# Fused attention and two feed-forward blocks: row loads for the norms held behind key loads, queries loaded once to 64 partitions, and the second product of four more pairs in plain float32

## The chip, the cores and the metric

The program runs on one core of a Trainium2 chip. The metric is the device time of one execution in microseconds (us). An engine named PE here is TensorE (matrix products), DVE is VectorE, ACT is ScalarE, POOL is GpSimd, and SP is SyncE, whose queue issues every load and store of this kernel in program order.

## The reference, cut to what matters

```python
batch, n_heads, seq, head_dim = (4, 12, 448, 64)
q_n, k_n = rmsnorm(q, g_q), rmsnorm(k, g_k)          # over head_dim
scores = q_n @ k_n.T / sqrt(head_dim)
attn = softmax(scores)                                # max taken off, sum + 1e-9
x = (attn @ v) -> (batch * seq, 768)
a, b = x @ w1, x @ w2                                 # 768 x 1024 each
x = ((a * b) @ w3) @ w_out                            # 1024 x 1024, 1024 x 768
h = x @ w_in                                          # 768 x 2048
out = (h * clip(h + 3, 0, 6) / 6) @ w_out2            # 2048 x 768
```

The weights arrive as 64-bit floats and are turned into 32-bit ones on the chip.

## The kernel before

**Precision.** A float32 product is made of "fp32r" parts: each operand is split into a rounded high part and the rest (low), and high·high, high·low and low·high are added up (`mm3`, L79 to L82; the three products are its lines L80, L81 and L82; I call the three together a triple). Splitting costs one ACT copy for the high part and one subtraction on DVE or POOL for the low part.

**Work of a pair.** The 48 heads are taken as 24 pairs, six to a batch. A pair has eight score steps: one product of queries and keys of 112 x 448 against both key parts (`score`, L536 and L537), then on DVE the scaling with the row maximum (`scale_max`, L543) and the sign change of the maximum (L550), then the exponential on ACT (L555). Eight steps later the scores are transposed (L562, four to a block of 128 keys), copied out of PSUM by ACT as high part (`thi`, L571) and by DVE as low part (`tlo`, L581), and multiplied with V (`pv`). `vsplit` (L524 ACT, L525 POOL) makes V's parts, so V's two parts and the scores' parts give [V-high, V-low] x high and x low (L614, L615; L602 for the block shared by both heads). `xcopy` (ACT) and `xadd` (L630, DVE) put the two column halves together, and `xout` (POOL) divides by the row sum.

**Full pairs.** For pairs in `FULL` nothing is split: V is loaded straight into the tile that TensorE reads (`load_v`, two buffers, tag `vo`), the scores' transposes are copied once (ACT), and one float32 product per block does the work (L610, and L596 for the shared block). `tlo`, `vsplit` and `xadd` return at once. Before, `FULL` holds pairs 0 and 1.

**Norms.** `load_nat` loads queries and keys row by row (tag `nat`, two buffers); `ssq` squares them (ACT, L436), `ssum` sums them (DVE, L442), and a chain of short DVE and ACT operations (L448 to L466) makes the factors of two pairs, which go to memory and come back spread over all partitions (`load_rb`). `load_q` loads the transposed queries, twice over on 128 partitions (tag `qr`), and `qhi` and `qlo` make the high part on partitions 0 to 63 and the low part on 64 to 127.

**Filler.** Between the score steps `fill` puts in products of the feed-forward part: first W' = w3·w_out (128 triples of 384 columns, 384 matmuls), then from about pair 9 on layer 1 and layer 2 of the batches that attention has finished (triples of 448 columns). `rate` says how much per step. Their weights go through `convert` (L135 ACT, L136, L138 and L141 DVE) and a split (ACT and POOL), with few buffers. After the 24 pairs comes the rest of the feed-forward part.

**What sets the order.** The program says in which step each piece is called (`at(t, ...)` with the offsets of `SHIFT`), but a scheduler at build time fixes the final order on each engine from its own estimates. `tc.issue_after` keeps an instruction behind another one on the same queue; it adds no wait for the data.

Of the kernel before, what the change touches and what calls it, by code (L numbers as in the profile page):

```python
# [12 lines left out]
F32 = mybir.dt.float32  # L13
# [3 lines left out]
AF = mybir.ActivationFunctionType  # L17
# [5 lines left out]
B, H, S, D = 4, 12, 448, 64  # L23
HP = H // 2
NP = B * HP
P = 128
# [9 lines left out]
NH = DM // 2  # L36
XB = 7
TAGS = ("s", "t", "v", "f")
FULL = (0, 1)
LG = 8  # L40
AHEAD = 3
K3 = 12
# [4 lines left out]
def fused_kernel(ctx: ExitStack, tc: tile.TileContext, nat, qT, kT, vin, gq, gk,  # L47
                 w12, w3t, wo, win, wo2, outT):
    nc = tc.nc
# [15 lines left out]
    G = gs[:, 2:3]  # L65
# [21 lines left out]
    def dma(out, src):  # L87
        return nc.sync.dma_start(out, src)
# [7 lines left out]
    def at(t, fn, *a):  # L96
        tasks[max(t + SHIFT.get(getattr(fn, "__name__", ""), 0), now[0])].append((fn, a))
# [304 lines left out]
    T = {}  # L402
    anchors = {}

    def attention(ap, rate):
        def full(i):
            return i in FULL

        def load_nat(i):
            if i < NP:  # L410
                T["nat", i] = ap.tile([CP, 4 * NC, D], F32, tag="nat", bufs=2, name="nat")
                a = T.get(("kl", i - 2))
                with ExitStack() as es:
                    if a is not None:
                        es.enter_context(tc.issue_after(a.ins))
                    dma(T["nat", i], nat[i].rearrange("p a b d -> p (a b) d"))

        def load_q(i):
            T["qr", i] = ap.tile([P, 2, S], F32, tag="qr", bufs=1, name="qr")
            dma(T["qr", i], qT[i])  # L420

        def load_k(i):
            T["kr", i] = ap.tile([P, 2, S], F32, tag="kr", bufs=1, name="kr")
# [78 lines left out]

        def qhi(i):
            T["Q", i] = q = ap.tile([P, 2, S], F32R, tag="Q", bufs=2, name="Q")
            nc.scalar.activation(q, T["qr", i], AF.Copy, scale=G)

        def qlo(i):
            a = slice(64, 128)
            q = T["Q", i]
            nc.vector.scalar_tensor_tensor(out=q[a], in0=T["qr", i][a], scalar=G[a, :], in1=q[a],  # L510
                                           op0=ALU.mult, op1=ALU.subtract)

        def ksplit(i):
# [133 lines left out]
        groups = {s: [s, s + 1] for s in range(0, NP, 2)}  # L647

        load_nat(0)
        load_nat(1)  # L650
        dma(gs[:, 0:1], gq)
        dma(gs[:, 1:2], gk)
        nc.vector.tensor_mul(G, gs[:, 0:1], gs[:, 1:2])
        load_q(0)
        load_k(0)
        open_wprime()
# [10 lines left out]
        first = ExitStack()  # L667
        first.enter_context(tc.issue_after(T["rbl"].ins))
        qhi(0)
        qlo(0)  # L670
        ksplit(0)
        for z in range(10):
            prep[0].step()
        load_q(1)
        load_k(1)
        for z in range(16):
            prep[0].step()
        load_nat(2)
        load_nat(3)

        for i in range(NP):
            t = 8 * i
            n = i + 1
            if n < NP:
                at(t, qhi, n)
                at(t + 1, qlo, n)
                at(t + 2, ksplit, n)
            at(t - 4, load_v, i)
            if i + 2 < NP:
                at(t + 3, load_q, i + 2)  # L690
                at(t + 5, load_k, i + 2)
            at(t + 1, vsplit, i)
            if i % 2 == 0 and i + 2 < NP:
                g = groups[i + 2]
                at(t, ssq, i + 2)
                at(t + 2, ssq, i + 3)
                at(t + 3, ssum, i + 2, g)
                at(t + 3, load_nat, i + 4)
                at(t + 4, ssum, i + 3, g)
                at(t + 4, load_nat, i + 5)  # L700
                at(t + 5, rms1, g)
                at(t + 6, rms2, g)
                at(t + 16, load_rb, i + 3)

            u = t + LG
            at(u + 2, rsum1, i)
            at(u + 6, xcopy, i, 0)
            at(u + 7, xadd, i, 0)
            at(u + 8, small1, i, None)
            at(u + 9, small2, i, None)  # L710
            at(u + 9, xcopy, i, 1)
            at(u + 10, xadd, i, 1)
            at(u + 13, xout, i)
            if i % 2 == 0 and i + 2 < NP:
                g = groups[i + 2]
                tasks[t + LG] = [z for z in tasks[t + LG] if z[0] is not small1]
                tasks[t + LG + 1] = [z for z in tasks[t + LG + 1] if z[0] is not small2]
                at(t + LG, small1, i - 1, g)
                at(t + LG + 1, small2, i - 1, g)

        t = -1
# [36 lines left out]
    with tc.tile_pool(name="att", bufs=2, side="left") as ap:  # L758
        attention(ap, rate)
# [45 lines left out]
    step, q = 0, 0  # L805
# [126 lines left out]
```

## Time and profile before

| | us |
|---|---|
| median of 3 runs (lowest, highest) | 1272.6 (1270.17, 1278.13) |
| the profiled execution, as timed | 1276.18 |
| span of its trace | 1274.3 |

| engine | busy us | share of the span | instructions |
|---|---|---|---|
| PE | 1183.1 | 93% | 5868 |
| PE weight loads | 1033.9 | 81% | 5868 |
| DVE | 795.1 | 62% | 1524 |
| ACT | 678.8 | 53% | 1305 |
| POOL | 463.6 | 36% | 292 |

The span counts from the first to the last instruction; the timed execution holds 1.9 us more around it. Shares are averages over stages with different limits, so the stages have to be read one by one. "PEclk" is the granted clock of TensorE as a share of its upper level, 2.4 GHz; its other level, 1.2 GHz, is 0.5. Busy time of PE counts overlapping matmuls once, and a matmul's own time is longer than the distance to the next start, so a price is read from starts. An fp32 matmul leaves two records in the trace, an fp32r one leaves one.

### The profile page before, as it was taken

Reading aid. Unit: us, or ns where it says so; the run is one execution under the profiler, and the core shown is the slowest. Engines: PE = TensorE matmul, PEld = TensorE weight load, DVE = VectorE, ACT = ScalarE, POOL = GpSimd, SP = SyncE. Lnnn points to the kernel's source line nnn. Section 1 sums busy time; section 2 is a strip of 40 time slices with the busy share of each in tenths; the row PEclk is TensorE's granted clock in tenths of the full one; section 3 lists DMA queues with packets and bytes.
Section 4 is the critical chain, followed back from the end, with each engine's and each line's share of the span. In section 5 each row is a group of like instructions: output and inputs, shape, how many; then the busy total and the mean of one; then the engine's idle time right before and its main releaser. Section 6 shows DMA issues by size and latency. Waiting matters only on the chain.

```text
span 1274.3 us, 16884 instructions
## 1 busy us (share of the span) xinstructions
PE 1183.1 (93%) x5868; PEld 1033.9 (81%) x5868; DVE 795.1 (62%) x1524; ACT 678.8 (53%) x1305; POOL 463.6 (36%) x292
## 2 busy tenths in 40 slices
PE   3587998888889999999999999889999999999998
PEld 2355987667668999999998998778999999999997
DVE  6989789989993578768643446994433343343332
ACT  5887667866783566766642223444533353344332
POOL 4334324624443112222111003445454454545542
PEclk9698998989999999999999999899999999999999
DMA  7898664666688666676349983450100020001001
GB/s 248 253 256 243 202 193 167 194 229 228 211 274 306 209 217 199 235 225 220 134 163 382 348 323 113 158 173 25 60 28 1 1 87 1 1 1 44 1 1 44
DMA packets 64693, 203.72 MB, mean 160 GB/s; under 512 B 8544, under 2 KB 25440, under 8 KB 64608
## 3 DMA queue, kind: packets, MB, share of 16 engines
q1 hardware_dynamic: 64608, 202.65, 48.2%
q8 instruction: 46, 0.75, 0.2%
q14 instruction: 39, 0.32, 0.1%
HBM read 173.93 MB, written 28.68 MB: 159 GB/s over the span
## 4 chain that ended last, share of the span: by engine, by line
PE 67%; DMA 11%; DVE 10%; issue 5%; ACT 3%; POOL 2%; SPq 1%; DVEq 0%; POOLq 0%; ACTq 0%
PE bank L80 8%; PE bank L82 8%; PE bank L81 8%; PE acc L81 6%; PE acc L82 6%; PE acc L80 5%; PE h L80 5%; PE h L81 5%; PE h L82 5%; PE bank L562 3%; DMA raw<-in_w_dram 2%; DVE wf L141 2%; DMA wr<-in_wo_dram 2%; PE bank L536 2%; PE bank L537 2%
## 5 line engine op out<-in xcount | busy, mean ns | idle before, releaser
L800 POOL TENSOR_TENSOR wis<-wf,wis 128x768 fp32r<-128x768 f32 x63 | 119.8, 1902 | 234.1 <-ACT wis L799 234.1
L872 DVE SCALAR_TENSOR_TENSOR u<-u,h 128x448 f32<-128x448 f32 x64 | 39.5, 618 | 217.3 <-ACT u L871 217.3
L800 POOL TENSOR_TENSOR wos<-wf,wos 128x768 fp32r<-128x768 f32 x64 | 119.0, 1860 | 103.6 <-ACT wos L799 103.6
L80 PE MATMUL bank<-xhl,ws 128*128 128x448 f32 x384 | 145.1, 378 | 7.7 <-ACT ws L285 6.3
L543 DVE CUSTOM_DVE_ANT_0 PP<-bank,rb,rq 112x448 f32<-112x448 f32 x192 | 129.1, 677 | 31.9 <-PE bank L537 27.4
L82 PE MATMUL bank<-xhl,ws 128*128 128x448 f32 x384 | 143.9, 375 | 4.9 <-POOL ws L287 4.9
L81 PE MATMUL acc<-g,wos 128*128 128x448 f32 x384 | 144.3, 376 | 3.8 <-DVE g L876 3.7
L555 ACT ACTIVATE PP<-PP,mx 112x448 f32<-112x448 f32 x192 | 127.4, 664 | 37.4 <-DVE mx L550 34.2
L80 PE MATMUL acc<-g,wos 128*128 128x448 f32 x384 | 138.5, 371 | 5.5 <-ACT g L875 5.5
L82 PE MATMUL acc<-g,wos 128*128 128x448 f32 x384 | 143.2, 373 | 0.0
L81 PE MATMUL bank<-xhl,ws 128*128 128x448 f32 x384 | 142.5, 371 | 0.1
L80 PE MATMUL h<-x2h,wis 128*128 128x448 f32 x378 | 139.0, 368 | 0.0
L81 PE MATMUL h<-x2h,wis 128*128 128x448 f32 x378 | 138.9, 368 | 0.0
L82 PE MATMUL h<-x2h,wis 128*128 128x448 f32 x378 | 137.5, 364 | 0.4 <-POOL wis L800 0.4
L876 DVE TENSOR_TENSOR g<-u,g 128x448 fp32r<-128x448 f32 x64 | 97.9, 1529 | 33.6 <-ACT g L875 33.6
L871 ACT ACTIVATE u<-h,half 128x448 f32<-128x448 f32 x64 | 40.4, 631 | 143.2 <-PE h L82 143.2
L536 PE MATMUL bank<-K,Q 128*112 128x448 f32 x192 | 78.3, 409 | 37.5 <-DVE mx L543 25.0
L562 PE MATMUL bank<-ident,PP 112*128 112x112 f32 x672 | 97.0, 267 | 11.8 <-DVE xl L581 10.2
L562 PEld LDWEIGHTS bank<-ident,PP 112*128 112x128 f32 x672 | 80.5, 145 | 33.8 <-DVE xl L581 13.3
L571 ACT ACTIVATE xh<-bank 128x448 fp32r<-128x448 f32 (+1 forms) x156 | 83.0, 537 | 43.3 <-PE bank L562 38.4
L581 DVE TENSOR_TENSOR xl<-bank,xh 128x448 fp32r<-128x448 f32 x142 | 87.1, 615 | 25.5 <-ACT xh L571 23.8
L799 ACT ACTIVATE wos<-wf 128x768 fp32r<-128x768 f32 x64 | 54.1, 846 | 86.9 <-PE acc L82 86.7
(126 smaller groups left out, 2763.5 us busy)
## 6 DMA issues: line engine op xcount, KB each, us to landing
ws<-w12d SPq DMA_DIRECT2D x48, 768.0 KB, 5.1
ws<-wpd SPq DMA_DIRECT2D x32, 768.0 KB, 4.2
raw<-in_w_dram SPq DMA_DIRECT2D x32, 384.0 KB, 4.3
w12d<-ws SPq DMA_DIRECT2D x16, 768.0 KB, 6.0
wr<-in_win_dram SPq DMA_DIRECT2D x16, 768.0 KB, 4.5
wr<-in_wo_dram SPq DMA_DIRECT2D x16, 768.0 KB, 6.6
nat<-in_nat_dram SPq DMA_DIRECT2D x24, 448.0 KB, 5.9
qr<-in_qT_dram SPq DMA_DIRECT2D x24, 448.0 KB, 6.4
```

The source lines that it names most:

```text
L80: nc.tensor.matmul(ps, lh, rh, start=first, stop=False)
L81: nc.tensor.matmul(ps, lh, rl, start=False, stop=False)
L82: return nc.tensor.matmul(ps, ll, rh, start=False, stop=last)
L536: nc.tensor.matmul(ps[:CP, :S], qs, k1[:, j, :], start=True, stop=False)
L543: anchors[8 * i + s].append(nc.vector.tensor_tensor_reduce(out=T["PP", i][:, c, sl], in0=ps[:CP, :S], in1=T["rb", i][:, sl], op0=ALU.mult, ...
L555: anchors[8 * i + s].append(nc.scalar.activation(v, v, AF.Exp, bias=T["m", i][:, 8 + s : 9 + s], accum_out=T["sum", i][:, s : s + 1]))
L562: nc.tensor.transpose(ps[:, c * CP : c * CP + CP], src[:, c, kb * P : kb * P + P], ident[:CP, :CP])
L571: nc.scalar.activation(hi, ps, AF.Copy)
L581: nc.vector.tensor_sub(lo, ps, hi)
L799: nc.scalar.activation(t[:, 0, :], wf[q], AF.Copy)
L800: nc.gpsimd.tensor_sub(t[:, 1, :], wf[q], t[:, 0, :])
L876: nc.vector.tensor_sub(g[:, 1, :], u, g[:, 0, :])
```

## The change

Four edits. `FULL` becomes `range(HP)`, so pairs 2, 3, 4 and 5 are also done in plain float32 (no V split, no low parts, no adding of halves). `load_nat` of a later pair is called three steps later and is put behind a key load on SP's queue; before, the key load it asked for had not been issued yet at that step, and the hold took effect only for pairs 2 and 3. The queries are loaded once, to 64 partitions, and `qlo` reads from partitions 0 to 63 and writes to 64 to 127.

```diff
-FULL = (0, 1)
+FULL = range(HP)
...
         def load_nat(i):
...
-                a = T.get(("kl", i - 2))
+                a = T.get(("kl", i - 2)) or T.get(("kl", i - 3))
...
-            T["qr", i] = ap.tile([P, 2, S], F32, tag="qr", bufs=1, name="qr")
-            dma(T["qr", i], qT[i])
+            T["qr", i] = ap.tile([D, 2, S], F32, tag="qr", bufs=1, name="qr")
+            dma(T["qr", i], qT[i][:D])
...
-            nc.scalar.activation(q, T["qr", i], AF.Copy, scale=G)
+            nc.scalar.activation(q[:D], T["qr", i], AF.Copy, scale=G[:D, :])
...
-            a = slice(64, 128)
             q = T["Q", i]
-            nc.vector.scalar_tensor_tensor(out=q[a], in0=T["qr", i][a], scalar=G[a, :], in1=q[a],
+            nc.vector.scalar_tensor_tensor(out=q[D:], in0=T["qr", i], scalar=G[:D, :], in1=q[:D],
                                            op0=ALU.mult, op1=ALU.subtract)
...
-                at(t + 3, load_nat, i + 4)
+                at(t + 6, load_nat, i + 4)
...
-                at(t + 4, load_nat, i + 5)
+                at(t + 7, load_nat, i + 5)
```

The scheduler makes another order out of this for the first sixteen pairs. Three places follow, two on SP's queue and one on PE, before and now; a row is the line, the operation, the tile written, the tiles read, and the size. In the changed kernel lines from 508 on have a number smaller by one.

On SP's queue, right after the loads of the first pair (`qr` queries, `kr` keys, `nat` rows for the norms, `raw` weights, `vo` V), before:

```order
L88 DMA qr<-in_qT_dram 128x896
L88 DMA kr<-in_kT_dram 128x896
L88 DMA nat<-in_nat_dram 112x1024
L88 DMA raw<-in_wo_dram 128x768
L88 DMA nat<-in_nat_dram 112x1024
L88 DMA raw<-in_w3t_dram 128x1024
L88 DMA vo<-in_v_dram 128x512
L88 DMA raw<-in_w3t_dram 128x1024
```

and now:

```order
L88 DMA qr<-in_qT_dram 64x896
L88 DMA kr<-in_kT_dram 128x896
L88 DMA raw<-in_wo_dram 128x768
L88 DMA raw<-in_w3t_dram 128x1024 x2
L88 DMA nat<-in_nat_dram 112x1024 x2
L88 DMA vo<-in_v_dram 128x512 x2
```

The rows for the norms of pairs 2 and 3 now stand behind three weight loads, and the query load has half the size.

Further down on SP's queue, where the row sums of pair 0 go out and come back (`rsd`, `rsb`), before:

```order
L88 DMA rsd_59<-rss_656 8x112 [waits DMAHW6_49,DVE_49]
L88 DMA raw_559<-in_wo_dram 128x768 [waits DMAHW7_49,Pool_49]
L88 DMA nat_2311<-in_nat_dram 112x1024 [waits DMAHW0_49,DVE_49]
L88 DMA rsb_659<-rsd_59 64x448 [waits DMAHW6_49,DMAHW1_49]
L88 DMA rsb_659<-rsd_59 64x448 [waits DMAHW2_49]
L88 DMA vr_817<-in_v_dram 128x512 [waits DMAHW3_49,Pool_49]
```

and now:

```order
L88 DMA vo_578<-in_v_dram 128x512 [waits DMAHW7_49,PE_49]
L88 DMA rsd_59<-rss_653 8x112 [waits DMAHW0_49,DVE_49]
L88 DMA rsb_656<-rsd_59 64x448 [waits DMAHW1_49,DMAHW0_49]
L88 DMA raw_641<-in_w3t_dram 128x1024 [waits DMAHW2_49,Pool_49]
L88 DMA rsb_656<-rsd_59 64x448 [waits DMAHW3_49]
L88 DMA raw_698<-in_w3t_dram 128x1024 [waits DMAHW4_49,Pool_49]
```

The V load of pair 2 now goes to the tile that TensorE reads and waits for TensorE, ahead of the row sums and of weights of W'; the same holds for pairs 3 to 5. Before, pair 2's V had been loaded much earlier into a tile of its own (`vr`), and later loads of that tile wait for POOL.

On PE, behind the 116th to 117th score step (pair 14; `abh` and `ws` are data and weights of layer 2, the rest is attention), before:

```order
L537 MATMUL bank<-K,Q 112x448
L614 MATMUL bank<-xh,vo 128x448
L615 MATMUL bank<-xl,vo 128x448
L562 MATMUL bank<-ident,PP 128x112 x4
L80 MATMUL bank<-abh,ws 128x448
L81 MATMUL bank<-abh,ws 128x448
L82 MATMUL bank<-abh,ws 128x448
```

and now:

```order
L536 MATMUL bank_4138<-K_3973,Q_3773 112x448
L535 MATMUL bank_4168<-K_3972,Q_3773 112x448 [waits DVE_49]
L536 MATMUL bank_4168<-K_3973,Q_3773 112x448
L561 MATMUL bank_4109<-ident_69,PP_3740 128x112 [waits DVE_49]
L561 MATMUL bank_4109<-ident_69,PP_3740 128x112 x3
L614 MATMUL bank_4085<-xl_4046,vo_3734 128x448
L613 MATMUL bank_4085<-xh_4079,vo_3734 128x448 [waits Activation_49]
L535 MATMUL bank_4199<-K_3972,Q_3773 112x448 [waits DVE_49]
```

Before, the last row opens a block of 54 triples of filler between two score steps; now no filler stands there, and the block (59 triples) comes eight score steps later, in pair 15.

## Rows read from the trace of the kernel before

**Rows 1.** Windows of five stages: span, busy us of each engine, PEclk, DMA share, GB/s.

```profile
0.00:91.00 91.00, 53.92 (x196) 32.45 (x197) 76.84 (x178) 64.10 (x128) 34.80 (x29) 0.87 0.86 252
91.00:239.20 148.20, 130.17 (x671) 110.38 (x669) 130.51 (x318) 108.83 (x232) 53.70 (x37) 0.91 0.70 212
239.20:374.10 134.90, 116.24 (x569) 93.24 (x569) 125.18 (x294) 96.37 (x222) 62.95 (x47) 0.92 0.65 214
374.10:457.00 82.90, 80.17 (x426) 71.30 (x425) 42.48 (x107) 43.56 (x94) 20.98 (x16) 1.00 0.75 252
457.00:1274.30 817.30, 802.55 (x4013) 726.51 (x4011) 420.12 (x630) 365.90 (x633) 291.13 (x164) 0.99 0.35 122
```

**Rows 2.** The same windows, L537 alone (one per score step): PE, PE loads, PEclk, DMA.

```profile
0.00:91.00 91.00, 10.90 (x24) 5.51 (x24) 0.87 0.86 252
91.00:239.20 148.20, 19.10 (x49) 9.21 (x48) 0.91 0.70 212
239.20:374.10 134.90, 14.77 (x41) 7.12 (x40) 0.92 0.65 214
374.10:457.00 82.90, 5.83 (x17) 2.80 (x16) 1.00 0.75 252
```

**Rows 3.** Windows, shorter ones, columns as in the first group.

```profile
100.00:120.00 20.00, 15.24 (x57) 11.65 (x58) 18.54 (x46) 14.86 (x32) 7.21 (x6) 0.74 0.87 240
120.00:140.00 20.00, 15.24 (x76) 14.00 (x75) 15.62 (x31) 13.44 (x28) 6.88 (x5) 0.83 0.85 261
140.00:160.00 20.00, 20.00 (x121) 18.39 (x120) 16.00 (x38) 14.91 (x31) 7.35 (x5) 1.00 0.52 158
374.10:434.00 59.90, 57.17 (x297) 50.47 (x296) 24.97 (x64) 28.34 (x62) 16.41 (x13) 1.00 0.80 268
```

**Rows 4.** Groups by form, 91 to 239.2 us: busy us, mean ns | idle before.

```profile
L581 DVE TENSOR_TENSOR xl<-bank,xh 128x448 fp32r<-128x448 f32 x37 | 22.7, 615 | 1.7 <-ACT xh L571 1.5
L442 DVE TENSOR_REDUCE ss<-nat 112x16 f32<-112x1024 f32 x10 | 11.8, 1207 | 0.0
L436 ACT ACTIVATE nat<-nat 112x1024 f32<-112x1024 f32 x11 | 11.6, 1056 | 7.2 <-DMA nat<-in_nat_dram 7.2
L136 DVE TENSOR_SCALAR raw<-raw 128x512 int32<-128x512 int32 x12 | 10.1, 842 | 1.6 <-DMA raw<-in_w3t_dram 1.6
L630 DVE TENSOR_TENSOR xs<-bank,xs 64x448 f32<-64x448 f32 x10 | 6.1, 612 | 0.3 <-ACT xs L622 0.2
L448 DVE TENSOR_SCALAR ss<-ss 112x32 f32<-112x32 f32 x5 | 1.9, 383 | 0.0
```

**Rows 5.** Timeline of PE, 78 to 100 us: start, us, instruction (float32 products).

```profile
80.89 0.96 PE L610 MATMUL bank<-xh,vo 128*64 128x448 f32 x2
81.78 0.44 PE L81 MATMUL bank<-woh,w 128*128 128x384 f32 x1
...
87.64 0.97 PE L596 MATMUL bank<-xh,vo 64*64 64x448 f32 x4
88.54 0.46 PE L536 MATMUL bank<-K,Q 128*112 128x448 f32 x1
```

**Rows 6.** Timeline of PE, 176 to 184 us (split products, scores, W').

```profile
180.15 0.55 PE L562 MATMUL bank<-ident,PP 112*128 112x112 f32 x4
180.46 0.45 PE L615 MATMUL bank<-xl,vo 128*128 128x448 f32 x1
180.75 0.36 PE L536 MATMUL bank<-K,Q 128*112 128x448 f32 x1
180.95 0.36 PE L537 MATMUL bank<-K,Q 128*112 128x448 f32 x1
181.15 0.34 PE L80 MATMUL bank<-woh,w 128*128 128x384 f32 x1
181.33 0.34 PE L81 MATMUL bank<-woh,w 128*128 128x384 f32 x1
```

**Rows 7.** Timeline of PE, 384 to 392 us (a triple and the next score).

```profile
388.36 0.36 PE L80 MATMUL bank<-xhl,ws 128*128 128x448 f32 x1
388.57 0.36 PE L81 MATMUL bank<-xhl,ws 128*128 128x448 f32 x1
388.76 0.36 PE L82 MATMUL bank<-xhl,ws 128*128 128x448 f32 x1
388.97 0.37 PE L536 MATMUL bank<-K,Q 128*112 128x448 f32 x1
```

**Rows 8.** Waits of SP's queue: waiting line, releaser, us in total, times, longest us.

```profile
SPq L88 <- POOL vo L525: 24.2, 15, 4.5
```

**Rows 9.** DMA issues: times, KB each, median us from issue to landing.

```profile
wpd<-wst SPq DMA_DIRECT2D x48, 128.0 KB, 3.9
rsb<-rsd SPq DMA_DIRECT2D x48, 112.0 KB, 3.7
```

## The prediction

> **What bounds the kernel now.** I read the windows first, cut where a group of pairs has had its last score [rows 1]. How many score steps lie in each is the count of L537 [rows 2]: 24, 48, 40 and 16 (the instruction on a cut is counted on both sides), and the last 64 behind them. So stage 0 is pairs 0 to 2 (91.0 us), stage 1 pairs 3 to 8 (148.2), stage 2 pairs 9 to 13 (134.9), stage 3 pairs 14 and 15 (82.9), stage 4 the rest (817.3). The reader is to see in [rows 1] which engine is full in each. In stage 1 DVE is busy 130.5 of 148.2 us (88%) and in stage 2 125.2 of 134.9 (93%), with PE waiting in both and its granted clock at 0.91 and 0.92. In stage 3 DVE has 42.5 of 82.9 and PE 80.2 at clock 1.00; in stage 4 PE has 802.6 of 817.3. The first 374 us are thus DVE's, the rest PE's. The shorter windows [rows 3] show how evenly loaded engines do: from 100 to 140 us PE, DVE and ACT are all at 13 to 19 of 20, and PE got a clock of 0.74 and 0.83 and was busy 15.2 of 20; from 140 to 160 it was busy 20.0 of 20 at 1.00.
>
> Counts of instructions below are from the order on each engine, which stands before a run; durations are from the rows. PE's prices are distances between starts at full clock: a float32 block 0.89 (80.89 to 81.78), the two half-height products of the shared block together 0.90 [rows 5]; four transposes 0.31, a split product 0.29, a score product 0.20, a W' matmul 0.18 [rows 6]; a triple of layer 1 or 2 0.61 (388.36 to 388.97) [rows 7].
>
> **The change, edit by edit.** *Plain float32 for pairs 2 to 5.* Per pair it removes seven low parts (615 ns) and two additions of halves (612 ns) from DVE [rows 4], 5.5 us, so 22 us over four pairs, and the V split from ACT and POOL. On PE a pair costs 6 x 0.89 + 0.90 = 6.2 us where the sixteen split products cost at most 16 x 0.29 = 4.6: at least 1.6 us more per pair. The copies by ACT stay.
>
> *Row loads later.* The squares and sums of later pairs go from stages 0 and 1 to later ones: 5 sums fewer in stage 0, 3 fewer in stage 1, at 1.207 us [rows 4]. In stage 4, where DVE is busy half the time, they cost nothing; if that cover were gone, some 7 us.
>
> *Queries on 64 partitions.* `qhi` and `qlo` have the same length per partition, so I take their time as unchanged. Each query load has 224 KB less. Put together with the row loads, the queue has moved 12.8 MB instead of 14.6 by the key load of pair 4. At stage 0's 252 GB/s [rows 1] this is 7 us of transfer, but DVE is busy 77 of 91 us there and gets no less to do: 5 sums fewer (-6.0), 9 weight conversions more (about +6.8). Against it, the rows for pairs 2 and 3 stand behind three weight loads (1.4 MB, 5.6 us). So stage 0 changes by -7 to +5; I take -2, near the DVE row.
>
> The Trainium skill (SBUF — State Buffer, "Door 1: The DMA port swizzle") says that a transfer to partitions 0 to 63 reaches only 8 of the 16 ports and so runs at about half the rate. In this trace 112 KB to 64 partitions landed in 3.7 us and 128 KB out of 128 partitions in 3.9 [rows 9], which shows no such loss at that size. By the rule a halved query load would take as long as the whole one did, stage 0 would give nothing, and the sum would be 2 us higher.
>
> **Stage 1.** DVE there loses 26 low parts (16.0 us), 8 additions (4.9), 3 row sums (3.6), 11 conversions (about 8, the longest is 842 ns) and 11 short operations of the norms (about 3, at up to 383 ns) [rows 4]: 130.5 - 35.5 = 95 us. ACT loses net some ten instructions, none above 1.056 us [rows 4], so it stays near 101 of its 108.8. PE at full clock has now 292 W' matmuls (52.6), 96 score products (19.2), 41 groups of transposes (12.7), float32 products of four pairs and the rest of pair 1's (27 x 0.89 + 4 x 0.90 = 27.6) and 24 split products (7.0): 119 us; the same count for before gives 116. The fullest engine goes from 130.5 (DVE) to 119 (PE): the gain is capped by PE, not by the 35 us that DVE is relieved of. If PE had no gap (as from 140 to 160 us) the stage would take 119; if it were as from 100 to 140 us, 15.2 of 20, it would take 119 / 0.76 = 157. At the 88% that the fullest engine reached before it would be 135. I take 138, since now three engines stand at 119, 101 and 95: a gain of 10.
>
> **Stage 2.** DVE's counts change by a handful of instructions of either sign: 0, give or take 4.
>
> **Stage 3.** Here the order decides. Layer 1 and 2 need weights that DVE, ACT and POOL convert while attention runs. Before, 71 triples of filler stand in pair 14 and 23 in pair 15; now 11 and 91, the block having moved one pair down. The same filler is done by the end of pair 15 in both (181 triples), but pair 14 is now one more pair at the pace of DVE, with PE waiting: 134.9 / 5 = 27.0 us. Pair 15 has 91 x 0.61 = 55.5, nine groups of transposes 2.8, 16 score products 3.2, 15 split products 4.4, together 65.9; PE's idle time in pair 14 before was 59.9 - 57.2 = 2.7 us [rows 3], so I take 68.6. Sum 95.6 against 82.9: 13 us lost. Bounds: a lighter pair of 22 us with no idle time gives +5; 30 us and PE's waits doubled, +19.
>
> **Stage 4.** The same instructions are left on PE on both sides: 0.
>
> **Sum.** On the profiled execution's span, 1274.3 - 2 - 10 + 0 + 13 = 1275.3. That execution was timed at 1276.2, 3.6 above the median of the runs, 1272.6; the change of +1 on the median gives 1273.6, say 1274.
>
> **Rivals.** *Faster: PE runs stage 1 without gaps.* For it: the window at 140 to 160 us, and DVE falling to 95 of some 120 us, so that the maxima that release score banks come sooner. Against it: in-order queues, and [rows 3] at 100 to 140. With stage 1 at 122 (-26), stage 3 at +10 and stage 0 at -2 the time is 1272.6 - 18 = 1255. It decides from about 126 in stage 1.
>
> *Slower: the V loads hold SP's queue.* The V loads of pairs 2 to 5 now wait until PE has read the V of two pairs earlier; behind the first of them stand the row sums of pair 0 (`xout` waits for them) and the w3 loads that W' needs. Before, SP's waits for the V tile were 24.2 us in 15 waits, the longest 4.5 [rows 8]. If each of the four holds the queue for 4.5 us and PE runs dry for as long, 18 us come on top of the sum: 1291. Against it: weights have four buffers of lead, and the loads stand near the step at which the tile comes free. It decides from about 3 us each.
>
> *The filler's delay is free.* If PE in pair 14 had nothing to lose because the block starts earlier within the pair, stage 3 costs +5 and the time is 1266: still within 1%.
>
> **Chances.** A gain in stage 1 that stage 3 takes back, whichever of the two is a little larger (1260 to 1286): 0.50, the last rival within it. PE without gaps: 0.26. The V loads: 0.24. One per cent is 12.7 us, about what a measurement can tell from no change; the two rivals lie beyond it, so faster 0.26, same 0.50, slower 0.24. The forecast's own range by its terms is 1260 to 1286; with cases on both sides, the range reaches some 3 us past the centre of each rival, 1252 to 1294, which leaves out about 0.10 on either side.
>
> **What would show it.** Stage 1 (score steps 25 to 72) at 138, DVE busy about 95, PE the fullest at a granted clock of 0.9 or more; at 126 or less the first rival holds, above 148 the second, with waits of SP for PE of over 3 us at V loads. Stage 3 (steps 113 to 128) at 96, the long run of triples behind step 124. Stage 4 unchanged within 3 us. The step most likely to fail is the 88% to 86% in stage 1, as no row shows these three loads side by side for so long; the next is the pace of pair 14.

## The result, and the profile after

| | before | changed kernel |
|---|---|---|
| median (lowest, highest), us | 1271.38 (1268.70, 1278.13) | 1288.99 (1284.20, 1290.18) |
| the profiled execution, as timed | 1276.18 | 1289.90 |
| span of its trace | 1274.3 | 1288.1 |

The ratio is 1.0123, with a 95% interval of 1.009 to 1.0156: slower by 1.2%. The time lies in the range that was given, but outside the likeliest case (1260 to 1286).

First the windows of the changed kernel, cut at the same score steps as [rows 1] and with its columns (span, busy us of each engine, PEclk, DMA share, GB/s). The last three rows are pair 14, pair 15, and pairs 16 to 19, the first four of stage 4.

```profile
0.00:95.60 95.60, 59.57 (x222) 38.81 (x223) 76.78 (x177) 60.70 (x124) 34.66 (x31) 0.91 0.72 218
95.60:231.30 135.70, 129.01 (x656) 93.61 (x654) 104.09 (x259) 99.02 (x216) 44.45 (x31) 0.99 0.62 191
231.30:368.20 136.90, 114.67 (x539) 88.80 (x538) 126.17 (x294) 98.82 (x221) 60.03 (x45) 0.90 0.62 198
368.20:465.50 97.30, 89.82 (x445) 78.55 (x445) 53.21 (x118) 47.38 (x103) 23.10 (x18) 0.95 0.74 251
465.50:1288.10 822.60, 804.53 (x4013) 725.40 (x4011) 421.40 (x643) 369.09 (x641) 291.24 (x164) 0.99 0.35 121
368.20:393.20 25.00, 21.01 (x99) 16.71 (x98) 23.80 (x56) 19.68 (x44) 8.04 (x6) 0.86 0.92 315
393.20:465.50 72.30, 68.81 (x347) 61.84 (x347) 29.41 (x63) 27.70 (x60) 15.06 (x12) 0.98 0.68 229
465.50:563.10 97.60, 94.54 (x514) 82.39 (x513) 72.71 (x178) 63.97 (x139) 24.20 (x17) 1.00 0.71 219
```

And pairs 16 to 19 of the kernel before:

```profile
457.00:548.20 91.20, 91.20 (x510) 82.58 (x509) 69.53 (x168) 61.28 (x134) 24.48 (x17) 1.00 0.66 218
```

Taken against [rows 1], the span grew by 13.8 us:

| stage | forecast | measured |
|---|---|---|
| 0, pairs 0 to 2 | -2 | +4.6 |
| 1, pairs 3 to 8 | -10 | -12.5 |
| 2, pairs 9 to 13 | 0 | +2.0 |
| 3, pairs 14 and 15 | +13 | +14.4 |
| 4, the rest | 0 | +5.3 |

Stages 1 to 3 came out within 3 us of the forecast each. Stage 0, which was to gain, and stage 4, which was to stay, lost 9.9 us together. Where they lost it shows in three more views. On DVE from 7 to 27 us the chain of norms (L448, L460 to L466, the copy of the factors L485) runs to the first `scale_max` (L543; L542 in the changed kernel). Columns: start, us, instruction, and idle time before it with its releaser. Before:

```profile
8.64 0.18 DVE L448 TENSOR_SCALAR ss<-ss 112x32 f32<-112x32 f32 x1
10.12 1.15 DVE L510 SCALAR_TENSOR_TENSOR Q<-qr,gs,Q 64x896 fp32r<-64x896 f32 x1 [1.30 <-ACT Q L505]
11.31 1.98 DVE L460 TENSOR_TENSOR rt<-ry 112x32 f32<-112x32 f32 x1
...
15.60 0.25 DVE L485 COPY rks<-bank 16x112 f32<-16x112 f32 x1
...
21.16 0.68 DVE L543 CUSTOM_DVE_ANT_0 PP<-bank,rb,rq 112x448 f32<-112x448 f32 x1 [0.59 <-DMA rb<-rkd]
```

In the changed kernel:

```profile
9.38 1.15 DVE L509 SCALAR_TENSOR_TENSOR Q<-qr,gs,Q 64x896 fp32r<-64x896 f32 x1 [0.82 <-ACT Q L505]
10.55 1.96 DVE L448 TENSOR_SCALAR ss<-ss 112x32 f32<-112x32 f32 x1
...
13.57 0.18 DVE L460 TENSOR_TENSOR rt<-ry 112x32 f32<-112x32 f32 x1
...
15.60 1.27 DVE L462 TENSOR_SCALAR rt<-rt 112x32 f32<-112x32 f32 x1
...
20.38 0.26 DVE L485 COPY rks<-bank 16x112 f32<-16x112 f32 x1
...
26.26 0.68 DVE L542 CUSTOM_DVE_ANT_0 PP<-bank,rb,rq 112x448 f32<-112x448 f32 x1 [5.16 <-DMA rb<-rkd]
```

`qlo` of the first pair (L509) now stands ahead of L448, and more weight conversions stand between L448 and L485 (eleven, before four). The copy comes 4.8 us later, and the first maximum 5.1 us. The store of these factors (`rkd`) heads SP's queue, and the loads behind it are held until it and the loads that read the factors back (`rb`) are issued. SP's longest wait in the first 30 us, before and in the changed kernel, is the one of this store (before, the wait is put down to a conversion that stands beside L485 on DVE):

```profile
SPq L88 <- DVE raw L136: 8.9, 1, 8.9
```

```profile
SPq L88 <- DVE rks L485: 13.4, 1, 13.4
```

The store and the first other load behind it, before:

```profile
15.88 0.33 SPq L88 DMA_DIRECT2D rkd<-rks  x1
...
20.18 0.35 SPq L88 DMA_DIRECT2D raw<-in_wo_dram  x1
```

and in the changed kernel:

```profile
20.66 0.33 SPq L88 DMA_DIRECT2D rkd<-rks  x1
...
22.95 0.38 SPq L88 DMA_DIRECT2D raw<-in_wo_dram  x1
```

The store is 4.8 us later, the load behind it 2.8 us. From 14.7 to 22.1 us of the changed kernel next to nothing moves (DMA share 0.00, 1 GB/s):

```profile
14.70:22.10 7.40, 1.43 (x4) 0.66 (x4) 6.40 (x14) 3.10 (x6) 5.03 (x4) 1.00 0.00 1
```

Before, the same window moved 129 GB/s:

```profile
14.70:22.10 7.40, 2.29 (x6) 1.18 (x7) 6.78 (x15) 3.26 (x6) 6.04 (x3) 1.00 0.46 129
```

These 129 GB/s are 0.95 MB in 7.4 us; by size most of it is the two loads of the factors (392 KB each), so the window shows their delay first and that of the other loads only at its end.

In pairs 16 to 19 of the changed kernel ACT's squares (L436) wait for late row loads, and DVE, whose order is fixed, stands behind the squares (waiting line, releaser, us in total, times, longest us):

```profile
DVE ss L442 <- ACT nat L436: 8.9, 2, 5.0
...
ACT nat L436 <- DMA nat<-in_nat_dram: 7.2, 3, 4.0
```

Before, neither wait is there, and PE was busy 91.20 of 91.20 us.

### The profile page after: what moved, and what is told of

Its sections match the earlier page's. It is cut to its first block, busy times and chain, and to the rows that moved or that the text cites. A ratio compares the mean times of both kernels' runs of the same rounds, so it can differ in the third digit from the quotient of the medians.

```text
span 1288.1 us, 16794 instructions
## 1 busy us (share of the span) xinstructions
PE 1197.6 (93%) x5868; PEld 1025.2 (80%) x5868; DVE 781.7 (61%) x1488; ACT 675.0 (52%) x1301; POOL 453.5 (35%) x288
## 4 chain that ended last, share of the span: by engine, by line
PE 56%; DMA 6%; DVE 6%; ACT 2%; issue 2%; POOL 0%; SPq 0%; ACTq 0%; DVEq 0%; POOLq 0%
PE bank L80 6%; PE bank L82 6%; PE bank L81 6%; PE acc L81 5%; PE acc L82 5%; PE acc L80 5%; PE h L80 5%; PE h L81 5%; PE h L82 5%; DMA wr<-in_win_dram 2%; PE bank L561 2%; DVE wf L141 2%; DMA wr<-in_wo_dram 2%; PE bank L535 1%; PE bank L614 1%
## 5 line engine op out<-in xcount | busy, mean ns | idle before, releaser
L542 DVE CUSTOM_DVE_ANT_0 PP<-bank,rb,rq 112x448 f32<-112x448 f32 x192 | 128.5, 674 | 29.3 <-PE bank L536 23.1
L80 PE MATMUL h<-x2h,wis 128*128 128x448 f32 x378 | 139.2, 368 | 0.0
L516 POOL TENSOR_TENSOR K<-kr,K 128x896 fp32r<-128x896 f32 x24 | 53.0, 2209 | 144.6 <-ACT K L515 137.8
```

The lines of the kernel that those rows point to most:

```text
L80: nc.tensor.matmul(ps, lh, rh, start=first, stop=False)
L516: T["ka", i] = nc.gpsimd.tensor_sub(k2, r, k1)
L542: anchors[8 * i + s].append(nc.vector.tensor_tensor_reduce(out=T["PP", i][:, c, sl], in0=ps[:CP, :S], in1=T["rb", i][:, sl], op0=ALU.mult, ...
```

## The experiments

All compare with the kernel before, run on the same chip. The table at the end of each group gives the spans of stretches in their profiled executions, from the start of one pair's eighth second score product to that of another's; "rest" reaches to the end of the span.

### Which edit costs the time

Two theories. A: stage 1's gain is taken back by the filler's delay, late row sums and the start. B: plain float32 is more work for PE, and that costs wherever it stands. The edits went in alone and in twos; F is plain float32 for pairs 2 to 5, N the later row loads, Q the halved query load.

**F alone**, `e1_full_only`:

```diff
-FULL = (0, 1)
+FULL = range(HP)
```

> Only pairs 2 to 5 in plain float32; loads as before. In its order the filler block stands in pair 15 (88 triples), as in the changed kernel. Theory A (the gain of about 12 us in pairs 3 to 8 is taken back by the block that comes a pair later, about +14 in pairs 14 and 15; nothing is lost behind pair 15): between -2 and +6 us to before, 1269 to 1277. Theory B (the added PE work of the four pairs, some 8 to 14 us, comes straight on top since PE bounds the program): +8 to +14, wherever the block stands.

Measured: 1277.27, ratio 1.002 (1.0004 to 1.0037). B falls: the extra work of PE costs at most 0.4%. A has its time, but not its terms. The late block is there (pairs 14 and 15: 87.0 us against 82.9, 4.1 more and not 14), pairs 9 to 13 gain 6.6, and pairs 3 to 8, which were to gain 12, gain nothing. Their window, columns as above:

```profile
95.70:243.70 148.00, 136.25 (x665) 99.54 (x664) 115.88 (x278) 104.83 (x226) 48.55 (x33) 0.95 0.67 201
```

DVE has 14.6 us less to do in it than before (130.51 in [rows 1]), and the stretch is as long.

**F and Q**, `e2_full_q64`: the changed kernel with the row loads as before.

```diff
-                a = T.get(("kl", i - 2)) or T.get(("kl", i - 3))
+                a = T.get(("kl", i - 2))
...
-                at(t + 6, load_nat, i + 4)
+                at(t + 3, load_nat, i + 4)
...
```

> Plain float32 for pairs 2 to 5 and the halved query loads, row loads as before. Here the scheduler leaves the filler block in pair 14 (74 triples). Theory A: pairs 14 and 15 take about 83 us as before, pairs 3 to 8 some 10 less, pairs 0 to 2 up to 4 more, pairs 16 on as before: -4 to -10 us, 1261 to 1267. Theory B: +8 to +14 as any kernel with the four pairs in plain float32.

Measured: 1283.94, ratio 1.0069 (1.0043 to 1.0096): slower, though the filler block is back in pair 14. A's gain is not there, and pairs 3 to 8 take 150.0 us, no less than before. B has its number, but F alone did not have it, so it is Q that adds.

**N alone**, `e3_nat_only`:

```diff
-                a = T.get(("kl", i - 2))
+                a = T.get(("kl", i - 2)) or T.get(("kl", i - 3))
...
-                at(t + 3, load_nat, i + 4)
+                at(t + 6, load_nat, i + 4)
...
```

> Only the later row loads. The block is split, 25 triples in pair 14 and 71 in pair 15, and four late row sums fall behind pair 15. Theory A: the late sums cost about +5 us behind pair 15 (DVE stands behind a row load that has not landed, PE behind DVE), pairs 14 and 15 as before within 4, pairs 3 to 8 some 5 less: 0 to +6 us in all. Theory B (the loss is PE's extra work alone): 0 within 3, and nothing behind pair 15.

Measured: 1277.26, ratio 1.0023 (1.0009 to 1.0037), which either theory allowed. Pairs 16 to 19 cost 2.2 us more, with the late rows waiting there. Pairs 3 to 8 gain 9.4 us and pairs 9 to 13 lose 6.5; the rest cancels. The window of pairs 3 to 8:

```profile
90.10:228.80 138.70, 123.73 (x651) 105.11 (x650) 122.23 (x297) 99.92 (x215) 54.89 (x36) 0.91 0.65 198
```

**Q alone**, `e4_q64_only`:

```diff
-            T["qr", i] = ap.tile([P, 2, S], F32, tag="qr", bufs=1, name="qr")
-            dma(T["qr", i], qT[i])
+            T["qr", i] = ap.tile([D, 2, S], F32, tag="qr", bufs=1, name="qr")
+            dma(T["qr", i], qT[i][:D])
...
```

> Only the halved query loads; the block stays in pair 14 (65 triples). Theory A: the first pair's norm chain stands behind weight conversions in DVE's new order, so the first eight scores end some 4 us later, and the rest is as before: 0 to +5 us. If the smaller loads relieve the queue in the first 91 us as forecast: -2 to -5.

Measured: 1286.47, ratio 1.0088 (1.0064 to 1.0111), 11.8 us and more than either case allowed. The edit that was costed at a small gain is the dear one.

**F and N**, `e5_full_nat`: the changed kernel with the queries loaded whole (the edit of Q undone).

```diff
-            T["qr", i] = ap.tile([D, 2, S], F32, tag="qr", bufs=1, name="qr")
-            dma(T["qr", i], qT[i][:D])
+            T["qr", i] = ap.tile([P, 2, S], F32, tag="qr", bufs=1, name="qr")
+            dma(T["qr", i], qT[i])
...
```

> The changed kernel with the query loads as before. Block in pair 15 (91 triples) and late row sums behind pair 15, but the first norm chain as before. Theory A: the loss of the changed kernel (+14 in its profile, +17 in its runs) less about 4 at the start: +9 to +14 us. Theory B: +8 to +14 too; the two part by stage: A has +14 in pairs 14 and 15, about -12 in pairs 3 to 8 and +5 behind pair 15.

Measured: 1272.45, ratio 0.9983 (0.9959 to 1.0008). Both A and B missed. Late block, later sums and plain float32 together cost nothing: the 134.1 us of pairs 3 to 8 pay for them.

**N and Q**, `e6_nat_q64`: the changed kernel with plain float32 for pairs 0 and 1 only.

```diff
-FULL = range(HP)
+FULL = (0, 1)
```

> The changed kernel with only pairs 0 and 1 in plain float32. Block split (25 triples in pair 14, 69 in pair 15), late row sums behind pair 15. Theory A: about +4 at the start, +5 behind pair 15, -5 in pairs 3 to 8: 0 to +7 us. Theory B: 0 within 3, because PE has no more work than before.

Measured: 1293.62, ratio 1.0146 (1.0102 to 1.0189). A and B missed again. Q adds 1.2% to N, as it adds 0.5% to F, 0.9% to nothing and 1.4% to both (differences of the ratios).

| pairs | 0 | 1-2 | 3-8 | 9-13 | 14 | 15 | 16-19 | 20-23 | rest |
|---|---|---|---|---|---|---|---|---|---|
| before | 33.2 | 57.5 | 148.1 | 135.0 | 59.8 | 23.1 | 91.2 | 91.0 | 635.4 |
| changed | 37.2 | 58.1 | 135.7 | 136.9 | 25.0 | 72.3 | 97.6 | 90.7 | 634.6 |
| F | 33.1 | 62.5 | 148.0 | 128.4 | 20.9 | 66.1 | 91.2 | 91.0 | 633.7 |
| F, Q | 36.7 | 61.5 | 150.0 | 130.5 | 63.3 | 23.1 | 91.2 | 91.0 | 635.6 |
| N | 32.6 | 57.5 | 138.7 | 141.5 | 27.8 | 55.5 | 93.4 | 91.3 | 635.1 |
| Q | 37.0 | 59.1 | 151.8 | 141.5 | 51.7 | 23.1 | 91.2 | 92.4 | 636.3 |
| F, N | 33.4 | 59.2 | 134.1 | 134.6 | 17.2 | 72.7 | 94.1 | 92.5 | 635.1 |
| N, Q | 37.0 | 57.7 | 145.1 | 141.6 | 33.8 | 51.5 | 97.1 | 90.3 | 635.9 |

All four kernels with Q take 3.6 to 4.4 us longer for pair 0 than their partners without it. With N they lose again in pairs 16 to 19. Pairs 3 to 8 gain with N (138.7, with F 134.1), and not with F alone.

### The load itself, or the order built from it

Q changes two things: the load, with the two operations that read it, and the order that the scheduler builds (which of its estimates moved it, no run shows). Theory C says order, D says load. The two can be parted, because the kernels with and without Q issue the same instructions: an edge from each instruction to its successor on the engine (issue order only, no wait) fixes the order of one in the other.

**The changed kernel in the order of F and N**, `e7_all_oldorder`:

```diff
...
+def keep_order(tc):
+    ...
+    for t in ORDER.values():
+        ...
+        for a, b in zip(row, row[1:]):
+            tc.add_manual_dep(b, a.name, mb.DependencyInfo(mb.DependencyClass.NoSync, mb.DependencyReason.DATA),
+                              reason="keep_order")
...
         fused_kernel(tc, *args)
+        keep_order(tc)
```

> All four edits as in the changed kernel, but every engine's instructions are pinned to the order that was built for the kernel with plain float32 and the later row loads and the whole query load (1272.5 us in its run); only the size of the 24 query loads and the two operations that read them differ from that kernel. Theory C, the halved load costs nothing itself and all of its 16 us come from the order that was built from it: 1272 +- 3, pair 0 at 33 to 34 us, pairs 16 to 19 at 94. Theory D, a load on 64 partitions is itself dear (its issue took 470 to 481 ns against 333, and it landed after 4.6 us for half the bytes): time as in the changed kernel, 1285 to 1290, pair 0 at 37. In between: both share.

Measured: 1271.86 against 1276.28, ratio 0.9967 (0.9952 to 0.9982). C holds, D falls: with the halved load in another order the whole loss is gone. Its windows, cut at the starts of the same score products (0.3 us ahead of the cuts above), and pairs 16 to 19 in the last row:

```profile
0.00:91.60 91.60, 57.12 (x231) 37.49 (x231) 77.15 (x176) 62.06 (x128) 38.95 (x31) 0.89 0.77 223
91.60:223.40 131.80, 127.89 (x647) 93.05 (x645) 103.92 (x260) 96.88 (x214) 43.85 (x30) 0.99 0.66 196
223.40:357.30 133.90, 113.25 (x551) 90.09 (x550) 126.76 (x300) 99.82 (x223) 61.02 (x46) 0.92 0.69 217
357.30:450.10 92.80, 86.14 (x433) 75.40 (x432) 49.63 (x112) 45.67 (x99) 22.67 (x17) 0.96 0.76 248
450.10:1267.60 817.50, 801.92 (x4014) 726.01 (x4012) 421.47 (x643) 369.61 (x641) 290.68 (x164) 0.99 0.36 122
450.10:541.20 91.10, 90.97 (x505) 81.60 (x504) 71.86 (x175) 64.37 (x140) 24.47 (x17) 1.00 0.74 228
```

With the same cuts, every stage is shorter than in the changed kernel, by 3.7, 3.9, 3.0, 4.5 and 5.4 us, with the same instructions and the same bytes. Its start, on DVE, is that of the kernel before:

```profile
8.64 0.18 DVE L448 TENSOR_SCALAR ss<-ss 112x32 f32<-112x32 f32 x1
9.62 1.15 DVE L509 SCALAR_TENSOR_TENSOR Q<-qr,gs,Q 64x896 fp32r<-64x896 f32 x1 [0.81 <-ACT Q L505]
...
15.09 0.25 DVE L485 COPY rks<-bank 16x112 f32<-16x112 f32 x1
...
20.62 0.68 DVE L542 CUSTOM_DVE_ANT_0 PP<-bank,rb,rq 112x448 f32<-112x448 f32 x1 [0.55 <-DMA rb<-rkd]
```

This is also the one version whose interval lies below the kernel before.

**Whole query load in the order of the changed kernel**, `e8_whole_neworder`: F and N as in `e5_full_nat`, and `keep_order` with the other order.

```diff
 ORDER = {
-    (the order of F and N)
+    (the order of the changed kernel)
...
-            T["qr", i] = ap.tile([D, 2, S], F32, tag="qr", bufs=1, name="qr")
+            T["qr", i] = ap.tile([P, 2, S], F32, tag="qr", bufs=1, name="qr")
...
```

> The reverse: queries loaded whole to 128 partitions, with every engine pinned to the order of the changed kernel. Theory C: as slow as the changed kernel, 1286 to 1291, pair 0 at 37, pairs 16 to 19 at 97 to 98; the row loads land no earlier. Theory D: 1272 to 1276, pair 0 back at 33. If the saved bytes themselves help, this is slower than the changed kernel by some us.

Measured: 1290.5, ratio 1.0116 (1.0076 to 1.0157): as slow as the changed kernel, though its queries are loaded whole. C holds from this side too. What the load is worth by itself is the difference between kernels of one order: 0.9967 against 0.9983, and 1.0123 against 1.0116; the intervals overlap both times, so it can't be told from nothing.

**The first norm chain ahead of the conversions**, `e9_chain_first`:

```diff
-                nc.vector.tensor_copy(sb[: 8 * n, :], ps[: 8 * n, P : P + CP])
+                T["rkc"] = nc.vector.tensor_copy(sb[: 8 * n, :], ps[: 8 * n, P : P + CP])
...
-        qlo(0)
+        with tc.issue_after(T["rkc"].ins):
+            qlo(0)
         ksplit(0)
-        for z in range(10):
-            prep[0].step()
+        with tc.issue_after(T["rkc"].ins):
+            for z in range(10):
+                prep[0].step()
```

> The changed kernel with one hold more: on DVE the low part of the first queries and the first ten steps of weight conversion stand behind the copy of the first norm factors, so the chain of short norm operations runs at once. Theory C: pair 0 falls from 37 to 33 us or below and the whole by 4 us, to 1283 to 1286, the rest as in the changed kernel (pairs 16 to 19 at 97 to 98). Theory D: pair 0 stays at 36 to 37, and the whole within 2 us of the changed kernel.

Measured: 1293.13, ratio 1.0125 (1.0089 to 1.0161). Pair 0 falls to 31.3 us, as C said, and the whole time does not follow (C had 1283 to 1286). The 5.9 us are given back right behind: pairs 1 and 2 take 63.8 us instead of 58.1. The two windows, of this kernel and of the changed one:

```profile
31.30:95.10 63.80, 48.54 (x187) 29.80 (x186) 56.98 (x134) 45.36 (x102) 24.54 (x19) 0.79 0.68 192
```

```profile
37.20:95.30 58.10, 45.75 (x190) 30.41 (x188) 53.40 (x130) 43.55 (x95) 23.17 (x19) 0.85 0.75 224
```

Both stretches end at 95 us. Within the first, from 40 to 60 us, DVE is full, the loads thin out to 106 GB/s and PE's clock is 0.50, its lower level; in the changed kernel, with DVE as full, these 20 us had 223 GB/s and 0.72:

```profile
40.00:60.00 20.00, 12.39 (x34) 7.81 (x33) 20.00 (x46) 14.05 (x33) 9.28 (x7) 0.50 0.38 106
```

```profile
40.00:60.00 20.00, 10.36 (x28) 4.96 (x26) 19.94 (x43) 17.09 (x35) 8.71 (x6) 0.72 0.75 223
```

The hold moved the conversions behind the chain, and the rest of the order was built anew around them; which of its moves cost the 5.7 us is open.

**The row loads of the last pairs early**, `e10_late_rows_early`:

```diff
-                a = T.get(("kl", i - 2)) or T.get(("kl", i - 3))
+                a = T.get(("kl", i - 2)) or T.get(("kl", i - 3)) if i < 16 else None
...
-                at(t + 6, load_nat, i + 4)
+                at(t + (3 if i >= 12 else 6), load_nat, i + 4)
...
```

> The changed kernel with the row loads of pairs 16 to 23 called at the earlier steps again and held behind nothing. If the late landing of these rows (ACT's squares waited 7 us for them, DVE 9 us for the squares) is what costs 6 us in pairs 16 to 19: these fall from 97.6 to 91 to 92, and the whole to 1282 to 1285 unless the sums of rows cost as much in pairs 9 to 13, where DVE is the fullest (eight sums at 1.2 us at most 10 us). If those waits cost PE nothing, pairs 16 to 19 stay at 96 to 98.

Measured: 1289.94, ratio 1.0106 (1.0076 to 1.0136). The waits for rows in pairs 16 to 19 are gone, PE is full, and the stretch falls to 91.2 us, as expected:

```profile
473.60:564.80 91.20, 91.20 (x510) 82.53 (x509) 69.28 (x169) 61.74 (x134) 24.70 (x17) 1.00 0.66 207
```

So the late rows, in this order, are what stage 4 lost by. But the whole time stayed, as it was allowed for if the sums cost as much in pairs 9 to 13: pairs 9 to 13 now take 141.4 us, with DVE busy 132.09 (126.17 in the changed kernel), since these squares and sums stand there again. Up to pair 9 the two kernels have one order on PE, and yet this execution came out of pair 9 at 258.1 us and the changed kernel's at 253.8, its clock in pairs 0 to 2 being 0.83 against 0.91. So two executions of one order differ by some 4 us there, and a smaller difference of one stretch between two profiles says little by itself.

```profile
234.30:375.70 141.40, 114.62 (x532) 87.05 (x531) 132.09 (x308) 103.20 (x229) 58.88 (x43) 0.92 0.68 213
```

| pairs | 0 | 1-2 | 3-8 | 9-13 | 14 | 15 | 16-19 | 20-23 | rest |
|---|---|---|---|---|---|---|---|---|---|
| changed | 37.2 | 58.1 | 135.7 | 136.9 | 25.0 | 72.3 | 97.6 | 90.7 | 634.6 |
| in the order of F, N | 32.5 | 59.1 | 131.8 | 133.9 | 17.8 | 74.9 | 91.1 | 91.4 | 635.0 |
| whole load, new order | 36.4 | 57.9 | 136.4 | 139.2 | 23.9 | 73.6 | 97.1 | 91.3 | 635.4 |
| chain first | 31.3 | 63.9 | 137.3 | 137.1 | 25.7 | 75.3 | 94.8 | 91.3 | 634.2 |
| late rows early | 38.3 | 60.8 | 135.2 | 141.4 | 23.6 | 74.3 | 91.2 | 91.2 | 634.6 |

### Which queue's order

C1 says the order of the loads on SP's queue, C2 that of the engines. Both kernels have all four edits and the same `keep_order`, with the two orders mixed.

**SP in the new order, the engines in that of F and N**, `e11_only_SP_new`:

```diff
 ORDER = {
-    'SP': (the order of F and N)
+    'SP': (the order of the changed kernel)
```

> All four edits; SP's queue pinned to the order of the changed kernel, the four engines to the order that made 1272 us. Theory C1, the loss comes from the order of the loads on SP's queue (row loads behind the key loads of two pairs later, weights and V in other places): 1284 to 1290, pairs 16 to 19 at 96 to 98 us because the rows land late. Theory C2, it comes from the order of the engines (DVE above all, where the first norm chain stands behind conversions): 1268 to 1275, pair 0 at 32 to 34, pairs 16 to 19 at 91 to 94. If both share, some 1278 to 1282.

Measured: 1319.39, ratio 1.0361 (1.0329 to 1.0393).

**SP in the order of F and N, the engines in the new one**, `e12_only_SP_old`:

```diff
 ORDER = {
     'SP': (the order of F and N)
-    'PE', 'DVE', 'Activation', 'Pool': (the order of F and N)
+    'PE', 'DVE', 'Activation', 'Pool': (the order of the changed kernel)
```

> The reverse: SP's queue pinned to the order that made 1272 us, the four engines to that of the changed kernel. Theory C1: 1268 to 1275. Theory C2: 1284 to 1290, pair 0 at 36 to 38. If both share, some 1278 to 1282.

Measured: 1338.82, ratio 1.0506 (1.046 to 1.0553). Both theories missed, and by more than the whole effect: either mixture is far worse than either order. Pairs 0 to 2 take 106.1 us in the former and 110.6 in the latter (95.3 in the changed kernel), pairs 9 to 13 153.1 and 160.5 (136.9). Waits in the first 450 us of the former (ACT for rows, 8.1 us in the changed kernel) and of the latter (DVE for weights, 7.1 in the changed kernel):

```profile
ACT nat L436 <- DMA nat<-in_nat_dram: 31.0, 8, 10.0
```

```profile
DVE raw L136 <- DMA raw<-in_w_dram: 23.5, 10, 7.5
```

The question was put wrongly. Each of the two orders works as a whole, and here the loss can't be laid to one queue by swapping it.

## Why the prediction was right and wrong

**Stage 1 was right in its number**, -12.5 for -10. The work counted for PE (119 us) stands at 88% of 135.7 us, the share that the fullest engine had before; DVE fell to 104 instead of 95 and PE is the fullest, at clock 0.99. The faster rival needed 126 or less; the clock and the fullness were there, the last ten us were not. That the gain came by the step it was put down to, plain float32 taking work off DVE until PE caps it, is not shown. `e1_full_only` takes that work off DVE (130.5 to 115.9 us) and gains nothing in these pairs, 148.0 us; PE's work there, counted from its trace at the same prices, is about 121 us, 82% of the stretch and not 88%. The gap to 88% is some 10 us, more than the 4 us by which two executions of one order differed. The later row loads, which the prediction costed here as three row sums (3.6 us), gain 9.4 us by themselves (`e3_nat_only`), and both together 14.0 (`e5_full_nat`). Why plain float32 pays there only beside the later rows is open.

**Stage 3 was right in its number**, +14.4 for +13: pair 14 takes 25.0 us (27.0 was assumed) and pair 15 72.3 (68.6), the 59 triples behind step 124. But with the late block in another order the stage loses less: 7.0 us in `e5_full_nat`, whose pair 14 takes 17.2, and 4.1 in `e1_full_only`. That is near the +5 of the rival in which the delay is free. The pace of pair 14 was taken from a mean over five pairs, and the order decides it.

**The slower rival came true in its sign, not by its mechanism.** The V loads were to hold SP's queue for PE, 4.5 us four times, with stage 1 above 148. In stage 1 of the changed kernel SP waited for PE's reading of V twice, 4.4 us together, and the stage gained. By the forecast's own border of one per cent the result is slower, which had 0.24, all of it for this mechanism; and the upper end of the range, 1294, was drawn from it. That 1289 lies inside is luck. SP's wait:

```profile
SPq L88 <- PE bank L609: 4.4, 2, 3.9
```

**Stage 0 was wrong: -2 became +4.6**, just inside the bounds it was given (-7 to +5). The step that failed is the one on queries on 64 partitions; without them, in `e5_full_nat`, pairs 0 to 2 take 1.9 us more than before. It costed 224 KB less at 252 GB/s and the time of `qhi` and `qlo`. The latter is right: `qlo` took 1613 ns in the median, before 1635. The load is, by `e7_all_oldorder`, worth nothing that can be told. What the step left out is that the scheduler builds another order with this edit. The first norm chain now stands behind `qlo` and among eleven conversions; the prediction took the number of conversions from DVE's order and not their place. Pair 0's loss, 4.0 us, is that chain (`e9_chain_first` takes it away); the first maximum is 5.1 us late. And it delays more than DVE: the loads behind the store of the factors start 2.8 us later.

**Stage 4 was wrong: 0 became +5.3.** That the row sums "cost nothing" there held for their work, since DVE is busy 72.7 of 97.6 us in pairs 16 to 19. The step left out the wait: a sum whose rows land late stands in DVE's fixed order ahead of the next maxima. `e10_late_rows_early` takes that loss away. With the rows late but in another order (`e7_all_oldorder`) the stretch takes 91.1 (94.1 in `e5_full_nat`, of the same order), so lateness alone isn't enough for 97.6.

**The sum.** Plain float32 and later row loads alone are, by `e5_full_nat`, 1272.45 us, no change that can be told, which is what the sum of +1 said. In part this is luck: by stages their profile has +1.9, -14.0, -0.3, +7.0 and +4.2 us, for a forecast of -2, -10, 0, +13 and 0. The error is in the query load, which was given at most a small gain and cost 1.4% (0.9983 to 1.0123), some 17 us, by the order made for it. Shown: order, not load. Not shown: how much of the 20.5 us between the spans of the changed kernel and of `e7_all_oldorder` belongs to which place. Pair 0 (4.7 us, 36.4 to 38.3 in every kernel with that start, 31.3 to 33.4 in the others, the mixed `e11_only_SP_new` with 35.5 left aside) and pairs 16 to 19 (6.5) have a mechanism that an experiment removed, and both times the gain was lost elsewhere. For the 10.2 us in pairs 9 to 14 (161.9 against 151.7) no run shows one, and swapping SP's order did not tell it.

## What to carry to other kernels

An edit that changes a size or a place can change the order that a scheduler builds, far from the edit; read the order of every engine at the start and at the ends of waits before costing such an edit by its bytes. To part the two, fix the order of the one kernel in the other: here that turned a loss of 1.2% into a gain of 0.3%, with the same instructions and the same bytes. When edits are costed together, run each alone too: here the edit credited with the gain of stage 1 gained nothing there alone, and another one gained 9.4 us. And a mechanism that an experiment removes without moving the total was a place where time was lost, not the cause of the total.

## What the runs showed of the hardware

**The halved query load, to 64 partitions, took longer to issue.** The issue on SP's queue of the query load, kernel before, then the changed one (ns, smallest, median, largest):

```profile
L88 SPq DMA_DIRECT2D qr<-in_qT_dram x24: 327/333/1112, 2.6 to 575.5; - x24
```

```profile
L88 SPq DMA_DIRECT2D qr<-in_qT_dram x24: 470/481/542, 2.6 to 591.6; - x24
```

Half the bytes took 148 ns more to issue. In one and the same order they landed after 4.6 us (changed kernel) against 5.5 for the whole load (`e8_whole_neworder`), medians:

```profile
qr<-in_qT_dram SPq DMA_DIRECT2D x24, 224.0 KB, 4.6
```

```profile
qr<-in_qT_dram SPq DMA_DIRECT2D x24, 448.0 KB, 5.5
```

Half the bytes in 84% of the time: most of what halving could give was not there. The Trainium skill (SBUF — State Buffer, "Door 1: The DMA port swizzle") says that partitions 0 to 63 reach half the ports. By that rule, an estimate, both would land together; the rows lie between that and half the time. The two rows that the prediction set beside the rule (112 KB in 3.7 us, 128 KB in 3.9) are a load and a store of other sizes and tell less than this pair.

**A short DVE operation can last until POOL's beside it ends.** The first L448 takes 0.18 us in the kernel before; in the changed one it takes 1.96, from 10.55 to 12.51, while POOL's subtraction of the keys runs to 12.47:

```profile
10.29 2.18 POOL L516 TENSOR_TENSOR K<-kr,K 128x896 fp32r<-128x896 f32 x1 [8.98 <-ACT K L515]
15.17 1.66 POOL L203 TENSOR_TENSOR w<-raw,w 128x512 fp32r<-128x512 f32 x1 [2.70 <-ACT w L201]
```

L462 (0.18, now 1.27 from 15.60) ends within 0.1 us of POOL's next instruction, 15.17 to 16.83, in the same way. In the kernel before one operation of the chain (L460) was caught so, in the changed one three (L466 took 1.29 too). The Trainium skill (SBUF — State Buffer, "Who interferes with whom") calls the port that the two share an exclusive lock; these rows agree.

**Busy time of PE is not work.** The changed kernel and `e7_all_oldorder` have the same 5868 matmuls. PE's busy time is 1197.6 and 1186.3 us; the idle time, 90.5 and 81.3 us, differs less. So 11.3 us of the larger sum are not more work.
